# Pooled attention and a cosine-routed expert layer on one core: the expert chosen from the batch's mean value, and the work moved between passes and engines

## The chip, the cores and the metric

The kernel runs on one core of a Trainium2 chip. A core has five engines with queues of their own: TensorE (PE in the rows; its weight loads are PEld), VectorE (DVE), ScalarE (ACT), GpSimd (POOL) and SyncE (SP); transfers between HBM and the core's memory run on 16 DMA engines. The metric is the device time of one execution in microseconds (us), lower is better.

## What is computed

```python
def _attn_ref(q, k, v):                       # (8, 8, 576, 64)
    k_p = k.reshape(B, H, Sp, pool, D).mean(axis=3)      # pool = 8, Sp = 72
    v_p = v.reshape(B, H, Sp, pool, D).mean(axis=3)
    attn = softmax(scale * q @ k_p.T)
    return attn @ v_p
...
def _moe_ref(x, expert_emb, tau, w1, w2):     # x (4608, 512), 8 experts, F = 1024
    logits = xn @ en.T / tau                  # xn, en: rows of unit length
    expert_idx = np.argmax(logits, axis=1)
    gate_w = probs[np.arange(N), expert_idx]
    for e in range(E):
        mask = expert_idx == e
        h = np.maximum(x[mask] @ w1[e], 0.0)
        out[mask] = gate_w[mask, None] * (h @ w2[e])
```

The output of the attention, with the eight heads side by side, is the x of the expert layer. All inputs and the output are float32 in HBM; the loads turn them into fp16.

## The kernel before

**Batches and passes.** The work goes batch by batch, eight batches of 576 tokens. For each batch there is attention, and then one expert pass: all 576 tokens go through the one expert that the kernel takes for the batch's main one. `expert` (L299 to L317) routes tokens, counts which expert has most of them, and loads that expert's weights. Tokens of other experts would be handled in a loop at the end of the program (`For_i` and `If`), one more pass for each pair of batch and expert that the flags `pos_all` and `eb_all` show.

**Attention.** `kproc` (L158 to L172) adds neighbouring keys and transposes them, `qtr` (L181) transposes half of the queries, `vadd` (L190 to L195) adds groups of eight values into `vpx`; all three are VectorE's. `score` (L207, L213) is eight matmuls on TensorE and two exponentials on ScalarE; there are four a batch. `pv` (L227) is 48 small matmuls, `xtr` (L239 to L244) divides and transposes on VectorE into `xt_all`; there are three of each. `route` (L275 to L293) makes the logits and compares them on VectorE. `square` (L252, ScalarE), `sumsq` (L257, GpSimd), `ssq` (L265, six one-column matmuls, and a copy L269) and `norm` (L355, GpSimd) give the length of each token, and `prob` and `gate` (L359 to L378) the gate weight.

**Expert pass.** `hgrp` (L396) makes one of eight groups of the hidden layer in 8 matmuls of 288 columns; ScalarE brings it out of PSUM with a ReLU (L403), the sixth group VectorE (L405). `yblk` (L414) makes blocks of 128 tokens in 8 matmuls each, `ylast` (L437) the last 64 tokens. Blocks go out by VectorE (L427) and ScalarE (L425) in turn, the halves of the last one by one each (L443, L445). SyncE stores them (L469).

**Order.** Each engine works through its own queue in program order. The program order is made by `astream`: steps of all batches with a position in passes, sorted, and issued between the groups of the expert passes wherever the position is below `lead(b + done / total)`. Attention of a batch thus runs one to two passes ahead of its expert pass. All loads are issued by GpSimd, in order: inputs of a batch by `load_qkv` (L93 to L95, kk, qq, vv) from `more`, two batches ahead, and the two weight halves w1 and w2 by `load_w` (L100, L103) once the expert's index can be read. Input tiles have two buffers, weight tiles three, PSUM four.

Of the kernel before, what the change touches and what calls it, by code (L numbers as in the profile page):

```python
# [26 lines left out]
def kernel(  # L27
# [23 lines left out]
    NC = 5  # L51
# [45 lines left out]
    def load_w(e_val):  # L97
        w1 = wpool.tile([128, 4, F], FP16, name="w1")
        w2 = wpool.tile([128, 4, 2, DM], FP16, name="w2")
        nc.gpsimd.dma_start(  # L100
            out=w1,
            in_=moe_w1[ds(e_val, 1)].squeeze(0).rearrange("(p w) f -> p w f", w=4))
        nc.gpsimd.dma_start(  # L103
            out=w2,
            in_=moe_w2[ds(e_val, 1)].squeeze(0).rearrange(
                "(w p r) d -> p w r d", p=128, r=2))
        return w1, w2
# [42 lines left out]
    def attn_steps(b):  # L150
# [151 lines left out]
        def expert(cs, nfill=0):  # L302

            pc = psum()
            fill(pc[:, 512:704], nfill)
            count(cs, pc)
            mx = rt.tile([128, E], FP32, name="mx")
            nc.vector.max(out=mx, in_=pc[:, 0:E])
            ix = rt.tile([1, E], U32, name="ix")
            nc.vector.max_index(out=ix, in_max=mx[0:1], in_values=pc[0:1, 0:E])  # L310
            nc.vector.tensor_scalar(out=eb_all[:, b], in0=pc[:, 0:E], scalar1=mx[:, 0:1],
                                    scalar2=None, op0=ALU.is_ge)
            if len(cs) == NC:
                present(pc)
            e_val = nc.values_load(ix[0:1, 0:1], engines=[ENG.Pool], min_val=0,
                                   max_val=E - 1)
            weights[b] = load_w(e_val)  # L317
# [10 lines left out]

        routes[b] = st
# [17 lines left out]
        st['sumsq'], st['emit_ssq'] = sumsq, ssq
# [294 lines left out]
```

## Time and profile before

| | |
|---|---|
| median of 3 runs | 260.02 us (259.17 to 260.99) |
| the profiled execution | 259.8 us |
| its span, first to last instruction | 258.1 us |
| mean granted clock of TensorE | 0.915 |

A row of a group of instructions shows the line, engine, operation, output<-input, sizes and count; then busy time and mean duration of one (ns); then how long the engine stood idle ahead of them and which instruction ended most of that. A row of a stretch has its length, each engine's busy time (and count), the granted clock of TensorE (1.00 is 2.4 GHz, 0.50 is 1.2 GHz), the mean busy share of the 16 DMA engines and what they moved. A row of the chain has start, length and what ran. A row of the timeline has start, duration, engine, line and operation, and in brackets the idle time ahead and what ended it. A row of a load has the issuing engine, count, size as it lands and the time from issue to landing.

### The profile page before, as it was taken

To read this page: it belongs to the slowest core of one execution; us is meant where nothing else is said; L and a number is where in the kernel's file an instruction comes from. 1 tells how busy PE (TensorE), PEld (TensorE's weight loads), DVE (VectorE), ACT (ScalarE), POOL (GpSimd) and SP (SyncE) were. 2 spreads that over 40 slices of the span, in tenths; PEclk is the share of its full clock that TensorE was granted. 3 is DMA by queue.
4 is the path that set the end of the run, shared out by engine and by line. 5 is a ranking of instruction groups with operands and counts; after the bars stand their busy time and mean duration, and the time that the engine had idled before them with its cause. 6 is when DMAs were issued, how large, how long until landed. Compare 5 with 4: busy or idle time off the path is not lost.

```text
span 258.1 us, 6297 instructions
## 1 busy us (share of the span) xinstructions
PE 190.4 (74%) x2626; PEld 111.5 (43%) x2627; DVE 169.7 (66%) x361; ACT 107.4 (42%) x188; POOL 70.7 (27%) x75
## 2 busy tenths in 40 slices
PE   0235189096939986889598929898999999999930
PEld 0123146053416632664246603365556548657410
DVE  3774960977892989889967891989881494431210
ACT  3113129040637264548224633178339619325310
POOL 8204025042432126215430620116106113510000
PEclk9999999659977998899959986979999999999995
DMA  5998999879999738997999793239825965984140
GB/s 96 205 201 149 203 213 195 156 127 172 178 210 215 155 46 172 233 226 158 212 226 205 185 209 59 62 117 179 158 63 156 197 110 179 186 178 145 31 147 12
DMA packets 19583, 40.82 MB, mean 158 GB/s; under 512 B 2520, under 2 KB 8152, under 8 KB 18528
## 3 DMA queue, kind: packets, MB, share of 16 engines
q0 software_dynamic: 14096, 30.94, 65.9%
q1 hardware_dynamic: 5116, 8.86, 10.7%
q10 hardware_dynamic: 340, 0.59, 0.7%
q8 instruction: 21, 0.34, 0.5%
q14 instruction: 10, 0.08, 0.1%
HBM read 61.88 MB, written 9.44 MB: 276 GB/s over the span
## 4 chain that ended last, share of the span: by engine, by line
PE 37%; DVE 37%; DMA 12%; issue 4%; ACT 4%; POOL 1%; POOLq 0%; ACTq 0%
PE pa L396 15%; DMA vv<-in_v_dram 12%; PE pa L414 12%; DVE x_sb L241 6%; DVE xt_all L244 5%; DVE vv L190 4%; DVE vpx L195 4%; PE pa L227 3%; DVE kT L172 3%; DVE kk L158 3%; PE pa L437 2%; DVE qT L181 2%; PE pa L207 2%; PE pa L280 2%; DVE y_sb L427 2%
## 5 line engine op out<-in xcount | busy, mean ns | idle before, releaser
L396 PE MATMUL pa<-xt_all,w 128*128 128x288 f16 x512 | 74.2, 300 | 2.6 <-ACT y_sb L425 2.1
L414 PE MATMUL pa<-w,hT 128*128 128x512 f16 x256 | 66.6, 402 | 0.1
L396 PEld LDWEIGHTS <-w 128*128 128x128 f16 x512 | 49.9, 102 | 21.2 <-issue 6.0
L213 ACT ACTIVATE at<-pa 72x576 f16<-72x576 f32 x64 | 37.5, 643 | 27.8 <-PE pa L207 27.7
L403 ACT ACTIVATE hT<-pa 128x576 f16<-128x576 f32 x56 | 35.5, 648 | 16.6 <-PE pa L396 16.2
L207 PE MATMUL pa<-qT,kT 32*72 32x288 f16 x256 | 16.9, 330 | 30.1 <-DVE qT L181 13.1
L414 PEld LDWEIGHTS <-hT 128*128 128x128 f16 x256 | 23.3, 101 | 29.3 <-issue 8.3
L257 POOL TENSOR_TENSOR sq<-sq 128x1152 bf16<-128x1152 bf16 (+1 forms) x16 | 31.6, 1976 | 4.5 <-issue 3.8
L252 ACT ACTIVATE sq<-xt_all 128x576 bf16<-128x576 f16 x32 | 20.2, 673 | 25.8 <-DVE xt_all L244 24.9
L425 ACT ACTIVATE y_sb<-pa,gm 128x512 f32<-128x512 f32 x16 | 10.9, 683 | 45.8 <-DVE y_sb L427 40.5
L100 POOL DMA_DIRECT2D w<-in_moe_w_dram x8 | 4.8, 603 | 71.5 <-issue 23.8
L244 DVE STREAM_TRANSPOSE xt_all<-x_sb 128x768 f16<-128x768 f16 x24 | 23.5, 978 | 0.8
L207 PEld LDWEIGHTS <-kT 32*72 32x72 f16 x256 | 6.8, 116 | 39.6 <-issue 29.6
L241 DVE TENSOR_TENSOR x_sb<-pa,rc 128x768 f16<-128x768 f32 x24 | 23.0, 958 | 0.8
L355 POOL TENSOR_TENSOR ssq<-ssq,half_c 128x5 f32<-128x5 f32 x8 | 9.6, 1197 | 49.3 <-DVE ssq L269 49.3
L181 DVE STREAM_TRANSPOSE qT<-qq 128x1152 f16<-128x1152 f16 x16 | 21.7, 1362 | 0.0
L190 DVE TENSOR_TENSOR vv<-vv 72x2048 f16<-72x2048 f16 (+1 forms) x16 | 15.1, 947 | 9.3 <-DMA vv<-in_v_dram 9.0
L239 DVE RECIPROCAL rc<-pa 128x12 f32<-128x12 f32 x24 | 5.4, 226 | 22.7 <-PE pa L227 22.6
L227 PE MATMUL pa<-vpx,at 72*32 72x65 f16 x1152 | 15.6, 207 | 5.6 <-ACT y_sb L425 3.4
L227 PEld LDWEIGHTS <-at 72*32 72x32 f16 x1152 | 12.6, 104 | 14.6 <-issue 11.9
L427 DVE TENSOR_SCALAR y_sb<-pa,gm 128x512 f32<-128x512 f32 x16 | 11.7, 730 | 9.9 <-PE pa L414 9.9
L280 PE MATMUL pa<-enT,xt_all 128*128 128x8 f16 (+1 forms) x192 | 6.7, 172 | 14.8 <-DVE xt_all L244 14.6
(84 smaller groups left out, 159.5 us busy)
## 6 DMA issues: line engine op xcount, KB each, us to landing
w<-in_moe_w_dram POOLq DMA_DIRECT2D x16, 1024.0 KB, 11.8
out_dram<-y_sb SPq DMA_DIRECT2D x30, 256.0 KB
kk<-in_k_dram POOLq DMA_DIRECT2D x8, 576.0 KB, 12.0
vv<-in_v_dram POOLq DMA_DIRECT2D x8, 576.0 KB, 15.9
qq<-in_q_dram POOLq DMA_DIRECT2D x7, 576.0 KB, 12.4
out_dram<-y_sb SPq DMA_DIRECT2D x15, 64.0 KB
qq<-in_q_dram POOLq DMA_DIRECT2D x2, 288.0 KB, 8.1
out_dram<-y_sb ACTq DMA_DIRECT2D x2, 256.0 KB
```

What stands on the lines that cost most here:

```text
L181: nc.vector.transpose(out=qT.rearrange("p w r (t i) -> p t w r i", i=16), in_=qq.rearrange("p t (w r i) -> p t w r i", w=2, r=2))
L190: nc.vector.tensor_tensor(out=vv[:, :, 0:n], in0=vv[:, :, 0:n], in1=vv[:, :, n:2 * n], op=ALU.add)
L207: nc.tensor.matmul(out=pS[a // 2][0:G, (a % 2) * 512:(a % 2) * 512 + HALF], lhsT=kT[rows, w, r, :], rhs=qT[rows, w, r, :], start=(w == 0), ...
L213: nc.scalar.activation(out=at, in_=pS[i][0:G].rearrange("g (a c) -> g a c", a=2)[:, :, 0:HALF], func=AF.Exp, scale=escale)
L227: nc.tensor.matmul(out=px[ts(a, 32), c0:c0 + D + 1], lhsT=st['at', half, r, a // 2][:, a % 2, ts(blk, 32)], rhs=st['vpx'][:, 2 * a + r, 0: ...
L241: nc.vector.tensor_tensor(out=x_sb, in0=pxv[:, :, :, 0:D], in1=rc.unsqueeze(3).to_broadcast([128, 2, 6, D]), op=ALU.mult)
L244: nc.vector.transpose(out=xt_all[:, b].rearrange("p w (t l) -> p t w l", l=32)[:, ts(u, 6)], in_=x_sb.rearrange("p b j d -> p (b j d)").re ...
L252: nc.scalar.activation(out=st['sq'][:, w], in_=xt_all[:, b, w], func=AF.Square)
L257: nc.gpsimd.tensor_tensor(out=sq[:, 0:n], in0=sq[:, 0:n], in1=sq[:, n:2 * n], op=ALU.add)
L396: nc.tensor.matmul(out=ph[:, half * 512:half * 512 + HALF], lhsT=w1v[:, kk, w // 2, w % 2, :], rhs=xt()[:, kk, ts(half, HALF)], start=(kk ...
L403: nc.scalar.activation(out=dst, in_=src, func=AF.Relu)
L414: nc.tensor.matmul(out=py, lhsT=st['hT'][:, w // 2, w % 2, ts(c, 128)], rhs=w2[:, w // 2, w % 2, :], start=(w == 0), stop=(w == 7))
```

## The change

The main expert of a batch is no longer counted from routed tokens. `guess_sum` multiplies the summed values `vpx` by a column of ones (8 one-column matmuls), copies the sums over 128 columns, and `guess` multiplies them by the expert vectors (`enN`, 4 matmuls) and takes the largest. `weigh` then loads the weights. The routing of each token stays, as it makes the gate weights and the flags of the loop at the end. Positions are set by new tables: attention and routing inputs of batch b stand in pass b-1, the preparation of keys, queries and values in pass b-2, routing and gate of b at the start of pass b. `sumsq` is gone: `ssq` sums over the four parts by matmuls instead (24 a batch), and `square` makes 192 tokens of all four parts at once. All evacuations of the expert pass are on ScalarE, but for two blocks of the last batch. The hidden tile is split into two, the blocks of y are taken in a new order, and the first loads stand in a new order.

```diff
-    def load_w(e_val):
+    def load_w1(e_val):
         w1 = wpool.tile([128, 4, F], FP16, name="w1")
...
+    def load_w2(e_val):
         w2 = wpool.tile([128, 4, 2, DM], FP16, name="w2")
...
-        def square(w):
-            if w == 0:
-                st['sq'] = xp.tile([128, 4, S], BF16, name="sq", bufs=1)
-            nc.scalar.activation(out=st['sq'][:, w], in_=xt_all[:, b, w], func=AF.Square)
-
-        def sumsq():
-            sq = st['sq']
-            for n in (2, 1):
-                nc.gpsimd.tensor_tensor(out=sq[:, 0:n], in0=sq[:, 0:n], in1=sq[:, n:2 * n],
-                                        op=ALU.add)
...
             for c in (4, 0, 1, 2, 3):
-                for rows in token_rows(c):
-                    nc.tensor.matmul(out=pq[rows, c:c + 1],
-                                     lhsT=st['sq'][:, 0, cols(c)], rhs=ones_b,
-                                     start=True, stop=True)
+                for w in range(4):
+                    for rows in token_rows(c):
+                        nc.tensor.matmul(out=pq[rows, c:c + 1],
+                                         lhsT=st['sq'][:, w, cols(c)], rhs=ones_b,
+                                         start=(w == 0), stop=(w == 3))
...
+        def guess_sum():
+            pm = psum()
+            for h in range(H):
+                nc.tensor.matmul(out=pm[ts(h % 2, 64), h // 2:h // 2 + 1],
+                                 lhsT=st['vpx'][:, h, 0:D], rhs=ones_m[0:G, 0:1],
+                                 start=True, stop=True)
+            xb = rt.tile([128, 4, 128], FP16, name="xb")
+            (nc.scalar.copy if b < 2 else nc.vector.tensor_copy)(
+                out=xb, in_=pm[:, 0:4].unsqueeze(2).to_broadcast([128, 4, 128]))
+            st['xb'] = xb
+
+        def guess():
+            pg = psum()
+            for w in range(4):
+                nc.tensor.matmul(out=pg[:, 0:E], lhsT=st['xb'][:, w], rhs=enN[:, w, :],
+                                 start=(w == 0), stop=(w == 3))
             mx = rt.tile([128, E], FP32, name="mx")
...
+        def weigh():
+            weights[b] = load_w(chosen())
...
+        def square(u):
+            if u == 0:
+                st['sq'] = xp.tile([128, 4, S], BF16, name="sq", bufs=1)
+            cs = ts(u, 192)
+            nc.scalar.activation(out=st['sq'][:, :, cs], in_=xt_all[:, b, :, cs],
+                                 func=AF.Square)
...
-        L = [(-0.36, more)]
-        SC = [(0.28 + 0.12 * i, lambda h=i // 2, r=i % 2: score(h, r)) for i in range(4)]
...
+        L = [(d + 1.02, more)]
+        G_ = [(d + 1.12, guess_sum), (d + 1.18, guess)]
+        W = [(d + 1.185, weigh)]
...
+        SC = [(d + sd * i, lambda h=i // 2, r=i % 2: score(h, r)) for i in range(4)]
...
-            if w != 5:
-                nc.scalar.activation(out=dst, in_=src, func=AF.Relu)
-            else:
-                nc.vector.tensor_scalar(out=dst, in0=src, scalar1=0.0, scalar2=None,
-                                        op0=ALU.max)
+            nc.scalar.activation(out=dst, in_=src, func=AF.Relu)
...
-                if i % 2:
+                if i % 2 or not apart:
                     nc.scalar.activation(out=y_sb, in_=py, func=AF.Copy, scale=g)
...
+        order = [(0, 0), (1, 0), (0, 1), (1, 1), (2, 0), (3, 0), (2, 1), (3, 1)]
+        ysteps = [(0.87, lambda c=c, part=part: yblk(c, part)) for c, part in order]
+        ysteps.insert(2 if apart else 8, (0.87, ylast))
...
+    run(a0['K'], a0['Q'][:1], a0['S'][:2], a0['V'], a0['Q'][1:])
+    emb_transposed()
+    run(a0['G'])
+    e_val = routes[0]['chosen']()
+    w1 = load_w1(e_val)
+    nc.gpsimd.dma_start(out=qq1, in_=flat(q, 1))
+    weights[0] = w1, load_w2(e_val)
```

GpSimd's queue at the start of the program, before: the inputs of batch 1, then the index of batch 0 (`ix`), its two weight halves and the inputs of batch 2.

```order
L93 DMA kk_132<-in_k_dram 128x2304
L94 DMA qq_131<-in_q_dram 128x2304
L95 DMA vv_133<-in_v_dram 72x8x512
...
L315 TENSOR_LOAD ix_266
...
L100 DMA w1_279<-in_moe_w1_dram 128x4096
...
L103 DMA w2_280<-in_moe_w2_dram 128x4x1024
L93 DMA kk_314<-in_k_dram 128x2304
```

The same place of the changed kernel:

```order
L537 DMA vv_134<-in_v_dram 72x8x512
L538 DMA kk_133<-in_k_dram 128x2304
...
L326 TENSOR_LOAD ix_219
...
L96 DMA w1_234<-in_moe_w1_dram 128x4096
L561 DMA qq_132<-in_q_dram 128x2304
...
L103 DMA w2_237<-in_moe_w2_dram 128x4x1024
L90 DMA kk_322<-in_k_dram 128x2304
```

The first weight half stands ahead of the queries of batch 1 now; up to the second half the two queues hold the same loads.

GpSimd's queue in a middle pass, before: the two additions of the squares (`sq`), the inputs of batch 5, the power for the token lengths (`ssq`), and the index and weights of batch 2.

```order
L257 TENSOR_TENSOR sq_896<-sq_896 128x1152
L257 TENSOR_TENSOR sq_896<-sq_896 128x576
L93 DMA kk_1097<-in_k_dram 128x2304
L94 DMA qq_1096<-in_q_dram 128x2304
L95 DMA vv_1098<-in_v_dram 72x8x512
L355 TENSOR_TENSOR ssq_1183<-ssq_1183,half_c_97 128x5
L315 TENSOR_LOAD ix_1390
...
L100 DMA w1_1404<-in_moe_w1_dram 128x4096
```

A middle pass of the changed kernel (pass 2): the inputs of batch 5 and the weights of batch 3.

```order
L90 DMA kk_1542<-in_k_dram 128x2304
L91 DMA qq_1541<-in_q_dram 128x2304
L92 DMA vv_1543<-in_v_dram 72x8x512
L382 TENSOR_TENSOR ssq_1586<-ssq_1586,half_c_97 128x5
L326 TENSOR_LOAD ix_1649
...
L96 DMA w1_1664<-in_moe_w1_dram 128x4096
...
L103 DMA w2_1666<-in_moe_w2_dram 128x4x1024
```

The additions are gone, and the weights of a batch follow the inputs of the batch two further on.

VectorE's queue around the index of batch 3, before: the routing counts give the index (`mx`, `ix`), then come the value additions of batch 5.

```order
L308 MAX mx_1830<-pa_1823 128x8
L310 MAX_INDEX ix_1832<-mx_1830,pa_1823 1x8
L311 TENSOR_SCALAR eb_all_91<-pa_1823,mx_1830 128x8
L321 TENSOR_SCALAR pos_all_92<-pa_1823 1x8
L190 TENSOR_TENSOR vv_1098<-vv_1098 72x8x256
```

VectorE's queue around the index of batch 3 in the changed kernel:

```order
L194 TENSOR_TENSOR vv_614<-vv_614 72x8x256
L285 TENSOR_REDUCE lmax_1522<-pa_1495 128x5
...
L194 TENSOR_TENSOR vv_614<-vv_614 72x8x128
...
L199 TENSOR_TENSOR vpx_1527<-vv_614 72x8x64
L263 COPY ssq_1586<-pa_1561 128x5
L334 TENSOR_SCALAR pos_all_92<-pa_1598 1x8
L304 CAST xb_1616<-pa_1607 128x512
L316 MAX mx_1647<-pa_1642 128x8
L318 MAX_INDEX ix_1649<-mx_1647,pa_1642 128x8
```

The index now stands behind the value additions of its own batch instead of ahead of those of batch 5.

## Rows read from the trace of the kernel before

**Rows 1.** The page, busy us (share of the span) and instructions by engine

```profile
PE 190.4 (74%) x2626; PEld 111.5 (43%) x2627; DVE 169.7 (66%) x361; ACT 107.4 (42%) x188; POOL 70.7 (27%) x75
```

**Rows 2.** Chain that ended last, three pieces of it

```profile
23.16 21.76 DMA vv<-in_v_dram
44.95 1.23 DVE vv L190
...
247.39 0.69 ACT y_sb L425
```

**Rows 3.** Timeline: GpSimd's loads up to pass 1, and TensorE's first matmul there

```profile
37.88 0.85 POOL L95 DMA_DIRECT2D vv<-in_v_dram  x1
...
63.12 0.56 POOL L100 DMA_DIRECT2D w<-in_moe_w_dram  x1 [8.03 <-DVE rc L239]
...
72.77 1.14 PE L396 MATMUL pa<-xt_all,w 128*128 128x288 f16 x8 [1.53 <-ACT y_sb L425]
```

**Rows 4.** DMA issues: the loads issued at 37.88 and at 63.12

```profile
vv<-in_v_dram POOLq DMA_DIRECT2D x1, 576.0 KB, 15.7
...
w<-in_moe_w_dram POOLq DMA_DIRECT2D x1, 1024.0 KB, 8.6
```

**Rows 5.** Busy time by stage; at the end clock, DMA share, GB/s

```profile
23.10:53.60 30.50, 16.78 (x200) 9.96 (x201) 20.69 (x38) 10.45 (x19) 8.33 (x9) 0.89 0.99 182
58.00:71.80 13.80, 10.34 (x191) 5.38 (x190) 11.21 (x23) 4.16 (x7) 4.76 (x4) 1.00 0.98 180
72.77:81.00 8.23, 5.46 (x30) 3.19 (x30) 5.58 (x9) 3.92 (x7) 1.99 (x4) 0.59 1.05 205
108.00:118.00 10.00, 8.56 (x185) 6.46 (x183) 8.57 (x23) 6.10 (x12) 1.42 (x2) 1.00 1.03 222
108.00:136.00 28.00, 23.19 (x370) 13.16 (x369) 24.33 (x47) 13.56 (x24) 10.32 (x10) 0.88 1.00 208
193.45:214.75 21.30, 20.89 (x332) 12.59 (x329) 11.24 (x31) 13.13 (x25) 6.22 (x5) 1.00 0.72 156
231.16:247.40 16.24, 16.19 (x114) 10.03 (x112) 4.38 (x13) 6.88 (x13) 0.00 (x0) 1.00 0.32 99
```

**Rows 6.** Chain that ended last, one-column and eight-column matmuls, scores, hidden groups

```profile
84.57 0.31 PE pa L265 x6
...
91.54 0.78 PE pa L280 x24
...
198.37 0.37 PE pa L207 x8
...
231.22 7.95 PE pa L396 x64
```

**Rows 7.** Line 396, durations (min/median/max), first and last start

```profile
L396 PE MATMUL pa<-xt_all,w x512: 282/286/448, 37.5 to 238.9; 128*128 128x288 f16 x171
```

**Rows 8.** Groups by line, ScalarE and VectorE

```profile
L213 ACT ACTIVATE at<-pa 72x576 f16<-72x576 f32 x64 | 37.5, 643 | 27.8 <-PE pa L207 27.7
L403 ACT ACTIVATE hT<-pa 128x576 f16<-128x576 f32 x56 | 35.5, 648 | 16.6 <-PE pa L396 16.2
...
L252 ACT ACTIVATE sq<-xt_all 128x576 bf16<-128x576 f16 x32 | 20.2, 673 | 25.8 <-DVE xt_all L244 24.9 <-DVE z L370 0.8
...
L427 DVE TENSOR_SCALAR y_sb<-pa,gm 128x512 f32<-128x512 f32 x16 | 11.7, 730 | 9.9 <-PE pa L414 9.9
L425 ACT ACTIVATE y_sb<-pa,gm 128x512 f32<-128x512 f32 x16 | 10.9, 683 | 45.8 <-DVE y_sb L427 40.5 <-PE pa L414 5.3
...
L445 ACT ACTIVATE y_sb<-pa,gm 64x256 f32<-64x256 f32 x8 | 3.8, 469 | 7.2 <-DVE y_sb L443 7.0
```

**Rows 9.** Line 195, durations (min/median/max) of the value sum

```profile
L195 DVE TENSOR_TENSOR vpx<-vv x8: 420/422/3260, 14.2 to 172.7; 72x512 f16<-72x512 f16 x8
```

**Rows 10.** Timeline: GpSimd's additions and VectorE's value sum beside them

```profile
68.27 4.54 POOL L257 TENSOR_TENSOR sq<-sq 128x1152 bf16<-128x1152 bf16 x2 [3.81 <-issue]
...
68.87 2.47 DVE L195 TENSOR_TENSOR vpx<-vv 72x512 f16<-72x512 f16 x1
```

More of the change, by code (lines that the diff above doesn't have):

```diff
@@ L300, in count, with chosen @@
                                  rhs=oh_all[:, b, c], start=False, stop=(c == cs[-1]))
[L302 to L306, printed above, removed]
-            mx = rt.tile([128, E], FP32, name="mx")
[L308 to L317, printed above, removed]
+        def guess_sum():
[13 more added lines that the diff above has]
+                                 start=(w == 0), stop=(w == 3))
+            mx = rt.tile([128, E], FP32, name="mx")
+            nc.vector.max(out=mx, in_=pg[:, 0:E])
+            ix = rt.tile([128, E], U32, name="ix")
+            nc.vector.max_index(out=ix, in_max=mx, in_values=pg[:, 0:E])
+            ixf = rt.tile([128, 1], FP32, name="ixf")
+            nc.vector.tensor_copy(out=ixf, in_=ix[:, 0:1])
+            nc.vector.tensor_scalar(out=eb_all[:, b], in0=irow[:, 0:E], scalar1=ixf,
+                                    scalar2=None, op0=ALU.is_equal)
+            st['ix'] = ix
+        def chosen():
+            return nc.values_load(st['ix'][0:1, 0:1], engines=[ENG.Pool], min_val=0,
+                                  max_val=E - 1)
+        def weigh():
+            weights[b] = load_w(chosen())
         def present(pc):
@@ L379, in gate @@
             gates[b] = gm
-        return [st['sumsq'], st['emit_ssq'], norm, prob, gate]
+        return [st['emit_ssq'], norm, prob, gate]
     def ffn_steps(xt, get_w, get_gm, finish, apart=False):
@@ L442, in ylast @@
             g = get_gm()
-            nc.vector.tensor_scalar(out=y_sb[0:64, 0:DH], in0=py[0:64, 0:DH],
-                                    scalar1=g[0:64, 4:5], scalar2=None, op0=ALU.mult)
-            nc.scalar.activation(out=y_sb[64:128, 0:DH], in_=py[64:128, 512:512 + DH],
-                                 func=AF.Copy, scale=g[64:128, 4:5])
+            for r in range(2):
+                nc.scalar.activation(out=y_sb[ts(r, 64), 0:DH],
+                                     in_=py[ts(r, 64), r * 512:r * 512 + DH],
+                                     func=AF.Copy, scale=g[ts(r, 64), 4:5])
             finish(4, y_sb)
@@ L450, in ffn_steps @@
             steps.append((1.0, lambda w=w: hgrp(w)))
-        ysteps = [(0.87, lambda c=c, part=part: yblk(c, part))
-                  for c in range(4) for part in range(2)]
-        steps += [(0.87, ylast)] + ysteps if apart else ysteps + [(0.87, ylast)]
+        order = [(0, 0), (1, 0), (0, 1), (1, 1), (2, 0), (3, 0), (2, 1), (3, 1)]
+        ysteps = [(0.87, lambda c=c, part=part: yblk(c, part)) for c, part in order]
+        ysteps.insert(2 if apart else 8, (0.87, ylast))
+        steps += ysteps
         return steps
@@ L471, in store, with emb_transposed @@
         return finish
-    def emb_transposed(nfill):
-        pe = psum()
-        fill(pe[:, 512:704], nfill)
-        pe = pe.bitcast(FP16)
-        for w in range(4):
-            nc.tensor.transpose(out=pe[:, ts(w, E)], in_=emb_h[:, ts(w, 128)],
-                                identity=ident_h[:E, :E])
-        nc.vector.tensor_copy(out=enT, in_=pe[:, 0:4 * E].rearrange("p (w e) -> p w e", e=E))
+    def emb_transposed():
+        for i, dst in enumerate((enN, enT)):
+            pe = psum().bitcast(FP16)
+            for w in range(4):
+                nc.tensor.transpose(out=pe[:, ts(w, E)], in_=emb_h[:, i, ts(w, 128)],
+                                    identity=ident_h[:E, :E])
+            nc.vector.tensor_copy(out=dst,
+                                  in_=pe[:, 0:4 * E].rearrange("p (w e) -> p w e", e=E))
     with tc.manual_schedule():
@@ L491 @@
         nc.gpsimd.dma_start(out=qq0[:, 0:TH * D], in_=flat(q, 0)[:, 0:TH * D])
-        nc.gpsimd.dma_start(out=vv0, in_=grouped(v, 0))
-        nc.gpsimd.dma_start(out=qq0[:, TH * D:T * D], in_=flat(q, 0)[:, TH * D:T * D])
         nc.gpsimd.iota(icol, pattern=[[0, 1]], base=0, channel_multiplier=1,
@@ L497 @@
                        allow_small_or_imprecise_dtypes=True)
+        nc.gpsimd.dma_start(out=vv0, in_=grouped(v, 0))
+        nc.gpsimd.dma_start(out=qq0[:, TH * D:T * D], in_=flat(q, 0)[:, TH * D:T * D])
         nc.vector.tensor_scalar(out=ident_h, in0=irow, scalar1=icol, scalar2=None,
@@ L508 @@
             scalar1=-2.0 ** -14, scalar2=None, op0=ALU.mult)
-        nc.scalar.activation(out=emb_h, in_=emb, func=AF.Square, accum_out=emb_n)
+        nc.scalar.activation(out=emb_h[:, 0], in_=emb, func=AF.Square, accum_out=emb_n)
         nc.gpsimd.tensor_tensor(out=emb_n, in0=emb_n, in1=half_c[:E, 0:1], op=ALU.pow)
-        load_qkv(1)
+        qq1, kk1, vv1 = new_qkv(1)
+        nc.gpsimd.dma_start(out=vv1, in_=grouped(v, 1))
+        nc.gpsimd.dma_start(out=kk1, in_=flat(k, 1))
         nc.gpsimd.iota(pair_b, pattern=[[1, B], [0, E]], base=0, channel_multiplier=0)
@@ L557 @@
             for c, f in steps:
-                while j < len(astream) and astream[j][0] < lead(b + done / total):
+                while j < len(astream) and astream[j][0] < b + done / total + 1e-6:
                     astream[j][1]()
```

85 lines of the change are left out of this document (44 added, 41 removed).

## The prediction

> **What bounds the kernel now.** I read the busy line of the page first, then the chain that ended last, then the busy time by stage, then the timeline around the first loads. The profiled execution took 259.8 us: a span of 258.1 us and 1.7 us around it; the median of the three runs shown is 260.02 us. The sum below is made against the 259.8.
>
> TensorE is busy for 190.4 us and VectorE for 169.7 us of the span, ScalarE for only 107.4 [rows 1], so no engine fills it. The chain says where the rest is. It begins with transfers: a value load of 9.55 us, then one of 21.76 us that ends at 44.95, where VectorE's first value addition of batch 2 could begin [rows 2]. TensorE's next matmuls wait for what stands behind that addition in VectorE's order. The first matmul of expert pass 1 comes only at 72.77 [rows 3]. Its weights were issued at 63.12, as VectorE had to find the expert from finished attention first, and landed 8.6 us later, at 71.7 [rows 3, 4]. The last stages look otherwise: from 193.45 to 214.75 lies one whole pass with the attention of the next batch beside it, TensorE busy for 20.89 of 21.30 us at full clock; the last pass alone takes 16.24 us [rows 5]. So the end runs at TensorE's pace, while up to there late loads and VectorE's queue take time. Had all passes run as the last ones do, 72.77 plus six passes of 21.3 plus 16.24 plus the end (10.7 us after the last matmul, which ends at 247.39 [rows 2]) would make 227 us of span instead of 258.1.
>
> The loads have a bound of their own. Where the 16 DMA engines are full they move 182 GB/s (23.1 to 53.6 us, share 0.99), 180 (58 to 71.8), 208 (108 to 136) and at best 222 (108 to 118) [rows 5]; sizes are as they land, in half the width of what is read. A middle pass moves two weight halves of 1.049 MB, three inputs of 0.590 MB and 1.18 MB of output: 5.05 MB.
>
> **The change, part by part.**
>
> *Expert from the mean.* The expert's index now needs the values alone and no attention, so weights are asked for 0.8 pass before use, right behind the input loads of batch b+2. The index must be right, which no trace shows. Worked out from the reference's inputs, the mean value picks, in all eight batches, the expert that all 576 tokens pick; the nearest second is batch 2, 0.519 against 0.560. So no extra pass at the end. The chain it adds on TensorE is 12 small matmuls a batch. Six one-column matmuls take 0.31 us, 0.052 each, and 24 of eight columns 0.78 us [rows 6]: 0.6 us a pass.
>
> *First pass.* The preparation of batch 1, which stood inside batch 0's attention on VectorE, now comes behind it, and fewer bytes stand ahead of the first weight half. Pass 0 began at 37.5 us [rows 7]; I take 28 for it, an estimate, with 33 as the late end. With 22.8 us for a pass (below) it then ends near 51, at the latest 56. This decides nothing, as the next part shows.
>
> *Pass 1, set by the queue.* Before, everything up to the values of batch 3 (inputs 0 to 3 and weights 0) had landed at 37.88 + 15.7 = 53.6 us [rows 3, 4], with the DMA engines full all the way. The changed kernel puts the same bytes ahead of the first weight half of pass 1. Behind 53.6 come that half and about half of pass 0's output: 1.049 + 0.59 = 1.64 MB, 7.9 us at 208 GB/s. Pass 1 starts at 61.5, after a wait of TensorE of 5 to 10 us from the end of pass 0, and 11.3 us earlier than before (72.77).
>
> *Passes 1 to 4, set by the queue.* Each needs 5.05 MB: 24.3 us at 208 GB/s. TensorE needs less: the 21.30 us of the whole pass, plus 18 more one-column matmuls for the sum of squares (18 x 0.052 = 0.94, which GpSimd's additions did before), plus 0.6 for the mean: 22.8 us. So pass 5 starts at 61.5 + 4 x 24.3 = 158.7. That the queue has no gap I read from the order: the input loads wait only for VectorE's preparation of a batch two ahead, and cover the few us in which the index is found.
>
> *Passes 5 to 7, set by TensorE.* No inputs are left; 3.28 MB a pass need 15.8 us. Two passes, 22.8 and 22.2 (the latter without a mean): 45.0. The last pass: 16.24, plus 0.78 for routing, 1.24 for 24 one-column matmuls, 0.3 for the count: 18.6. The end stays 10.7, the rest around the span 1.7.
>
> **Sum: 61.5 + 97.2 + 45.0 + 18.6 + 10.7 + 1.7 = 234.7 us.** I take 235.
>
> *ScalarE takes VectorE's evacuations.* Per pass: 8 hidden groups (0.648), 8 exponentials (0.643), 4 blocks (0.683), 2 half blocks (0.469) and 3 squares; one of 768 elements is 0.83 by the slope between the 256- and 512-element rows from the 576-element row's 0.673 [rows 8]. With 0.3 for the gate that makes 16.7 us of 22.8: hidden, though not everywhere (see the rivals). VectorE loses eight hidden groups, 14 of 16 blocks at 0.730 us [rows 8], and the half blocks. Off the chain, I count it at nothing.
>
> *No GpSimd sums.* The value sum takes 0.42 us in the median, but up to 3.26 [rows 9]; one of 2.47 us began 0.60 us after a pair of GpSimd additions and ended inside it [rows 10]. This loss goes. VectorE then has some 18 us of work in a pass and is late nowhere, so this too is already in the 24.3 and not added.
>
> *A page against the queue's rate.* The saturated stretch moved 182 GB/s as landed, twice that as read [rows 5]. The Trainium skill, page "DMA: Bandwidth & Descriptors", section "Anatomy of one DMA — SWDGE (gpsimd) path", fits a transfer as about 2.0 us plus its bytes at 436 GB/s. By that, even counting bytes as read, a middle pass (7.73 MB in, 1.18 out) would need an estimated 20.4 us, less than TensorE, and rival B would be the forecast. This trace does not reach that rate in any full stretch, so I go by the rows.
>
> **The rivals.**
>
> *B, TensorE sets all passes.* If the queue holds 222 GB/s, a pass needs 22.7 us of it, TensorE's own 22.8. Then 61.5 + 5 x 22.8 + 22.2 + 18.6 + 12.4 = 228.7. For it: that rate stood for 10 us. Against: not for 28. Its lower end, with pass 1 at 59.4 (the weight half alone behind 53.6, at 182) and passes at 21.3 as before, is 59.4 + 127.8 + 17.6 + 12.4 = 217.2.
>
> *C, ScalarE sets the first half of a pass.* There a score group (0.37) and a hidden group (an eighth of 7.95, 0.99) give TensorE 1.36 us of work [rows 6] and ScalarE 2 x 0.643 + 0.648 = 1.93. If none of the 0.57 is caught up, four pairs cost 2.3 us a pass: 61.5 + 6 x 25.1 + 18.6 + 12.4 = 243. Against: four PSUM buffers, and hidden groups alone, which leave ScalarE 0.34 us each. The clock adds to this side: from 72.77 to 81.00, after TensorE's waits, the granted clock was 0.59, so mostly the lower level of 1.2 GHz, against 1.00 from 193 us on [rows 5]. The wait before pass 1 may cost a like stretch again.
>
> *D, the queue stays at 180 GB/s,* as from 58 to 71.8. A pass is 28.1 us: 61.5 + 112.4 + 45.0 + 18.6 + 12.4 = 249.9.
>
> *E, slower: the mean picks a wrong expert.* Every batch in which it does gets one more pass in the loop at the end, with nothing to hide it: weights 8.6 us to landing [rows 4], 16.24 of matmuls [rows 5], then up to 11.3 us to read 1.18 MB of output back and store it again at 208 GB/s: 25 to 36 us. From the first wrong batch it decides: 260 to 271. Here the change would not do what it says.
>
> *F, within 1%: the index comes late.* It now stands on VectorE behind its own batch's value additions, which wait for their load. If values land late, the weights are issued late into an empty queue; 4 us in each of six passes give 259. Against: these values are loaded a pass earlier than they are added.
>
> **Chances.** Forecast 0.47, B 0.22, C 0.13, D 0.11, E 0.03, F 0.04. All but E and F are faster than 257.4 us, so faster by over 1% (about what a measurement of this kernel can tell from no change) has 0.93, within 1% 0.04, slower 0.03. The range runs from just above B's lower end to D: 219 to 250.
>
> **What would show it.** Right: first expert matmul near 28 us, pass 1 near 61 behind a wait for its weights, passes 1 to 4 about 24 us apart with the DMA share near 1, then about 22.5, no GpSimd addition beside VectorE, no loop pass. Wrong: pass starts 22 to 23 us apart with no wait for weights (B); TensorE waiting for ScalarE in the first half of passes (C); DMA idle while TensorE waits for weights (F).

## The result, and the profile after

The changed kernel takes 237.47 us in the median of 4 runs (236.38 to 238.43), the kernel before 260.28 beside it: a ratio of 0.913 (95% interval 0.907 to 0.918). The forecast was 235.0, with a range of 219 to 250. The profiled execution took 237.07 us, of which the span is 235.4. (Of two kernels below, the one with both edits back and the kernel before with the edits alone, some executions were disturbed; the ratios leave these out.)

The busy line of the page, which answers to [rows 1]:

```profile
PE 188.3 (80%) x2862; PEld 115.9 (49%) x2863; DVE 140.8 (60%) x341; ACT 124.5 (53%) x212; POOL 40.0 (17%) x59
```

TensorE has 236 more instructions and is busy for 2.1 us less. VectorE lost 28.9 us and GpSimd 30.7. The chain that ended last (start, length, what ran), for [rows 2]:

```profile
3.03 9.33 DMA vv<-in_v_dram
...
44.24 15.88 DMA w<-in_moe_w_dram
...
92.57 15.91 DMA w<-in_moe_w_dram
...
116.89 19.19 DMA w<-in_moe_w_dram
```

The value load of 21.76 us is gone from it; the first one stays, with 9.33 us. From 44 us up to pass 4 it runs through three weight loads, which take 15.9 to 19.2 us from issue to use where [rows 4] had 8.6: they now stand in a full queue. TensorE's first expert matmuls of passes 1, 3 and 4 in the timeline (start, duration, in brackets the idle time ahead), for [rows 3], and three of VectorE's additions that end in the keys `kT`, for later:

```profile
60.16 2.10 PE L423 MATMUL pa<-xt_all,w 128*128 128x288 f16 x8 [8.51 <-DMA w<-in_moe_w_dram]
...
108.53 1.15 PE L423 MATMUL pa<-xt_all,w 128*128 128x288 f16 x8 [1.42 <-DMA w<-in_moe_w_dram]
...
136.12 1.14 PE L423 MATMUL pa<-xt_all,w 128*128 128x288 f16 x4 [4.68 <-DMA w<-in_moe_w_dram]
...
180.66 0.77 DVE L176 TENSOR_TENSOR kT<-k 128x128 f16<-128x128 f16 x3
```

Pass 1 starts at 60.16 instead of 72.77, and TensorE waits for weights there, as forecast. The stages (span of time, length, busy time and count of PE, PEld, DVE, ACT, POOL, granted clock, DMA share, GB/s), for [rows 5]: the wait before pass 1, passes 1 to 4, pass 5, pass 6, the last pass, and two short stretches behind waits.

```profile
51.65:60.16 8.51, 0.01 (x1) 0.00 (x0) 3.50 (x8) 0.64 (x2) 0.00 (x0) 0.75 1.08 232
60.16:161.15 100.99, 94.25 (x1420) 57.60 (x1421) 67.72 (x158) 60.49 (x104) 17.92 (x24) 0.90 1.00 204
161.15:184.23 23.08, 21.67 (x361) 13.61 (x358) 17.25 (x41) 15.21 (x27) 2.54 (x3) 1.00 0.71 159
184.23:205.93 21.70, 21.57 (x361) 13.46 (x358) 11.48 (x32) 15.20 (x27) 2.54 (x3) 1.00 0.71 153
205.93:222.82 16.89, 16.89 (x148) 10.68 (x145) 4.02 (x20) 7.59 (x13) 1.19 (x1) 1.00 0.23 70
59.00:62.00 3.00, 1.83 (x8) 1.04 (x8) 0.00 (x0) 0.00 (x0) 0.00 (x0) 0.50 1.09 236
137.00:140.00 3.00, 3.00 (x41) 1.68 (x39) 0.17 (x1) 1.74 (x3) 0.00 (x0) 0.50 1.09 206
```

In passes 1 to 4 the DMA engines are full (share 1.00, 204 GB/s). In the last three TensorE is busy for 60.1 of 61.7 us at full clock. Behind the waits of 8.51 and 4.68 us the granted clock stood at 0.50, which is 1.2 GHz. Last, the value sum of [rows 9] (minimum, median and maximum, ns):

```profile
L199 DVE TENSOR_TENSOR vpx<-vv x8: 420/422/423, 14.4 to 186.2; 72x512 f16<-72x512 f16 x8
```

The sum never takes more than 0.423 us now (3.26 before).

### The profile page after: what moved, and what is told of

Its sections match the earlier page's. It is cut to its first block, busy times and chain, and to the rows that moved or that the text cites. A ratio compares the mean times of both kernels' runs of the same rounds, so it can differ in the third digit from the quotient of the medians.

```text
span 235.4 us, 6749 instructions
## 1 busy us (share of the span) xinstructions
PE 188.3 (80%) x2862; PEld 115.9 (49%) x2863; DVE 140.8 (60%) x341; ACT 124.5 (53%) x212; POOL 40.0 (17%) x59
## 4 chain that ended last, share of the span: by engine, by line
PE 46%; DMA 30%; DVE 11%; ACT 4%; issue 3%; POOL 1%; POOLq 1%; ACTq 0%
DMA w<-in_moe_w_dram 22%; PE pa L423 21%; PE pa L437 12%; DMA qq<-in_q_dram 4%; DMA vv<-in_v_dram 4%; PE pa L211 3%; PE pa L231 3%; DVE qT L185 3%; PE pa L259 2%; PE pa L460 2%; ACT at L217 1%; DVE vv L194 1%; DVE xt_all L248 1%; DVE x_sb L245 1%; ACT hT L429 1%
## 5 line engine op out<-in xcount | busy, mean ns | idle before, releaser
L423 PE MATMUL pa<-xt_all,w 128*128 128x288 f16 x512 | 77.4, 303 | 14.9 <-DMA w<-in_moe_w_dram 14.6
L423 PEld LDWEIGHTS <-w 128*128 128x128 f16 x512 | 48.4, 102 | 33.8 <-DMA w<-in_moe_w_dram 14.9
L429 ACT ACTIVATE hT<-pa 128x576 f16<-128x576 f32 x64 | 41.4, 647 | 38.5 <-PE pa L423 38.5
L437 PE MATMUL pa<-w,hT 128*128 128x512 f16 x256 | 58.6, 380 | 0.1
L346 ACT ACTIVATE sq<-xt_all 128x768 bf16<-128x768 f16 x24 | 20.2, 843 | 29.5 <-DVE xt_all L248 27.1
L211 PE MATMUL pa<-qT,kT 32*72 32x288 f16 x256 | 16.8, 327 | 12.7 <-DVE qT L185 11.4
L448 ACT ACTIVATE y_sb<-pa,gm 128x512 f32<-128x512 f32 x30 | 18.9, 678 | 11.9 <-PE pa L437 11.9
L382 POOL TENSOR_TENSOR ssq<-ssq,half_c 128x5 f32<-128x5 f32 x8 | 10.5, 1306 | 81.8 <-DVE ssq L263 81.8
L263 DVE COPY ssq<-pa 128x5 f32<-128x5 f32 x8 | 1.3, 159 | 15.9 <-PE pa L259 15.9
L467 ACT ACTIVATE y_sb<-pa,gm 64x256 f32<-64x256 f32 x16 | 7.4, 464 | 2.3 <-PE pa L460 2.1
L460 PE MATMUL pa<-w,hT 128*64 128x256 f16 x128 | 8.5, 276 | 0.0
## 6 DMA issues: line engine op xcount, KB each, us to landing
w<-in_moe_w_dram POOLq DMA_DIRECT2D x16, 1024.0 KB, 15.4
qq<-in_q_dram POOLq DMA_DIRECT2D x7, 576.0 KB, 15.2
```

The costliest lines, as they stand in the source:

```text
L211: nc.tensor.matmul(out=pS[a // 2][0:G, (a % 2) * 512:(a % 2) * 512 + HALF], lhsT=kT[rows, w, r, :], rhs=qT[rows, w, r, :], start=(w == 0), ...
L346: nc.scalar.activation(out=st['sq'][:, :, cs], in_=xt_all[:, b, :, cs], func=AF.Square)
L423: nc.tensor.matmul(out=ph[:, half * 512:half * 512 + HALF], lhsT=w1v[:, kk, w // 2, w % 2, :], rhs=xt()[:, kk, ts(half, HALF)], start=(kk ...
L429: nc.scalar.activation(out=dst, in_=src, func=AF.Relu)
L437: nc.tensor.matmul(out=py, lhsT=st['hT', w // 4][:, (w // 2) % 2, w % 2, ts(c, 128)], rhs=w2[:, w // 2, w % 2, :], start=(w == 0), stop=(w ...
L448: nc.scalar.activation(out=y_sb, in_=py, func=AF.Copy, scale=g)
```

## The experiments

The total came out near the forecast. The open question was whether for the forecast's reasons: it put the whole gain down to the early expert and the load queue, and counted the two edits on engines (no evacuations on VectorE, no sums on GpSimd) at nothing. From here on "the two edits" are these. Two stretches of each profile are compared, passes 1 to 4 and passes 5 and 6, which in the changed kernel last 100.99 and 44.78 us (23.08 + 21.70).

### The two edits, without and with the rest of the change

First the kernel before with the two edits alone; its order of work and its choice of expert stay.

```diff
-            if w != 5:
-                nc.scalar.activation(out=dst, in_=src, func=AF.Relu)
-            else:
-                nc.vector.tensor_scalar(out=dst, in0=src, scalar1=0.0, scalar2=None, op0=ALU.max)
+            nc.scalar.activation(out=dst, in_=src, func=AF.Relu)
...
-            for n in (2, 1):
-                nc.gpsimd.tensor_tensor(out=sq[:, 0:n], in0=sq[:, 0:n], in1=sq[:, n:2 * n],
-                                        op=ALU.add)
+            pass
```

(Blocks of y go to ScalarE and the sum of squares to TensorE as in the change.)

> The kernel before with the two engine parts alone: all evacuations of the expert pass on ScalarE, sums of squares by 24 matmuls, no GpSimd additions; expert still from routing counts, order as before. Theory Q: 246 to 256 us: pass 1 still waits for weights that are asked for late (start near 70 us against 60), and the passes up to the fifth lose only VectorE's delays. Rival V: 240 us or less.

It took 243.88 us (242.78 to 247.93), 0.938 of before (0.932 to 0.944). That lies between the two ranges, but 6.2 of the whole change's 8.7% come without the early expert. Where, the stretch of passes 1 to 3 shows, first in the kernel before and then in this one:

```profile
72.77:169.86 97.09, 77.22 (x1172) 43.55 (x1172) 76.97 (x148) 44.03 (x78) 27.27 (x26) 0.88 0.82 168
```

```profile
71.82:153.55 81.73, 71.20 (x1244) 42.23 (x1245) 58.40 (x132) 49.15 (x89) 14.10 (x18) 0.98 0.96 202
```

Three passes are 15.4 us shorter. VectorE's 77.0 us of work become 58.4, and with VectorE on time the loads that wait for it are issued sooner. The first weight halves of passes 2, 3 and 4 are issued at 89.9, 112.7 and 133.8 us instead of 95.1, 119.1 and 144.4, and the DMA share goes from 0.82 to 0.96. Pass 1 still starts at 71.82 us. The whole change starts it 11.7 us earlier, at 60.16, and is 6.4 us faster than this kernel in the medians.

Then the other way round: the changed kernel with one edit undone, with the other, and with both. GpSimd's sums back (`sumsq` stands behind `square` again, `ssq` has six matmuls):

```diff
+        def sumsq():
+            sq = st['sq']
+            for n in (2, 1):
+                nc.gpsimd.tensor_tensor(out=sq[:, 0:n], in0=sq[:, 0:n], in1=sq[:, n:2 * n], op=ALU.add)
...
+        Z = [(pd + 0.285, sumsq)]
```

> The changed kernel with one part undone: GpSimd adds the squares again (2 additions a batch, right behind the last square) and TensorE's sum of squares has 6 one-column matmuls instead of 24. Theory Q (the load queue and TensorE set the end, VectorE has slack): 236 to 240 us, as VectorE's slower additions (15 us in all before) stay inside its slack and TensorE saves 18 x 0.052 = 0.9 us a pass in passes 5 to 7, the value sum again up to 3 us beside a GpSimd addition, pass 1 starting at 60 as now. Rival V (VectorE's relief carries the gain): 245 to 250 us.

243.95 us (243.34 to 245.42), ratio 0.940 (0.934 to 0.946), just under the range of V. VectorE's evacuations back (the sixth hidden group, every other block, half of the last):

```diff
-            nc.scalar.activation(out=dst, in_=src, func=AF.Relu)
+            if w != 5:
+                nc.scalar.activation(out=dst, in_=src, func=AF.Relu)
+            else:
+                nc.vector.tensor_scalar(out=dst, in0=src, scalar1=0.0, scalar2=None, op0=ALU.max)
...
-                if i % 2 or not apart:
+                if i % 2:
```

> The changed kernel with one part undone: VectorE again takes the sixth hidden group, two of four blocks and one half block of each pass, some 20 us of work in all. Theory Q: 235 to 240 us; VectorE goes from 141 to about 161 us busy and ScalarE from 124.5 to about 105, and neither is waited for. Rival V: 244 us or more, with TensorE waiting for VectorE's evacuations at pass ends.

247.25 us (246.1 to 248.06), ratio 0.951 (0.945 to 0.957), as V had it. Both back, by the two diffs together:

> The changed kernel with both engine parts undone (GpSimd sums and VectorE evacuations as before), so that the early expert and the new order stand alone. Theory Q: 237 to 244 us, pass 1 starting at 60 us, VectorE busy near 175 us. Rival V: 250 us or more.

Ratio 0.968 (0.961 to 0.975), as V had it, from executions of 250.8 and 252.27 us. Undoing the edits costs 6.5 us, 9.8 us and, both together, some 14. The early expert and the new order, which this last kernel has without the edits, bring 3.2%. No run parts the early expert from the new positions, the split hidden tile and the other smaller parts of the change. The stretches show where the loss lies, first with the sums back, then with the evacuations back, each time passes 1 to 4 and passes 5 and 6:

```profile
61.04:162.39 101.35, 93.10 (x1348) 56.16 (x1349) 73.69 (x156) 60.55 (x104) 33.42 (x32) 0.91 1.00 203
162.39:215.02 52.63, 46.25 (x680) 28.05 (x677) 33.52 (x74) 30.56 (x53) 12.45 (x10) 0.90 0.61 135
```

```profile
60.06:164.47 104.41, 97.49 (x1420) 59.02 (x1421) 75.15 (x171) 52.03 (x86) 17.92 (x24) 0.89 0.99 197
164.47:215.82 51.35, 48.02 (x716) 29.17 (x713) 35.60 (x83) 27.47 (x46) 5.09 (x6) 0.90 0.63 138
```

With the sums back, passes 1 to 4 take 101.35 us against 100.99: the full queue covers the loss. Passes 5 and 6 have no such cover and go from 44.78 to 52.63. With the evacuations back it is 3.4 and 6.6 us. In passes 5 and 6 the granted clock is 0.90 in both, 1.00 in the changed kernel. Most of the 6.6 us of the evacuations is not waiting: TensorE is idle there for 3.3 us instead of 1.5, but busy for 48.02 us instead of 43.24 with the same 716 instructions.

### What a GpSimd addition costs, and what a shared evacuation costs

Putting the sums back does two things: GpSimd's additions run beside VectorE, and the sums of squares wait for GpSimd. To part them, the same additions were put into a tile that nobody reads, while TensorE went on summing all four parts.

```diff
+        def scratch_sums():
+            sq, sc = st['sq'], att.tile([128, 2, S], BF16, name="sc", bufs=1)
+            nc.gpsimd.tensor_tensor(out=sc, in0=sq[:, 0:2], in1=sq[:, 2:4], op=ALU.add)
+            nc.gpsimd.tensor_tensor(out=sc[:, 0:1], in0=sc[:, 0:1], in1=sc[:, 1:2], op=ALU.add)
```

> The changed kernel with GpSimd's two additions of the squares put back, but into a tile that nobody reads; TensorE still sums over all four parts itself. Theory P (the additions hurt by what they do to VectorE's instructions beside them, keys' additions above all): most of the 6.5 us that putting the sums back cost comes again, 241 to 245 us, and the mean of the four additions that end in kT rises from 0.35 to 0.8 us or more. Rival S (what hurts is the wait of the sums of squares for GpSimd): 236.5 to 239 us.

246.49 us (244.77 to 247.17), ratio 0.947 (0.940 to 0.953): the additions alone cost 9.0 us, above even the range of theory P. That is more than the 6.5 us of the sums put back: there TensorE has 36 one-column matmuls fewer in passes 5 and 6, which take 52.63 us against 54.06 here, and the end was 1.9 us shorter. With the sums back TensorE also waited for GpSimd itself, twice and 4.3 us in all, but in passes 0 and 2, ahead of a wait for weights or under the full queue. The timeline of this kernel around one pass boundary, GpSimd's additions, then VectorE's queue and TensorE beside and behind them:

```profile
185.36 2.36 POOL L351 TENSOR_TENSOR sc<-sq 128x1152 bf16<-128x1152 bf16 x1 [10.11 <-ACT sq L346]
...
185.50 0.78 DVE L167 STREAM_TRANSPOSE k<-ks 128x576 f16<-128x576 f16 x1
...
186.31 3.14 DVE L176 TENSOR_TENSOR kT<-k 128x128 f16<-128x128 f16 x3
...
187.80 1.30 POOL L352 TENSOR_TENSOR sc<-sc 128x576 bf16<-128x576 bf16 x1
...
193.03 0.18 DVE L285 TENSOR_REDUCE lmax<-pa 128x5 f32<-128x40 f32 x1
...
193.61 0.90 PE L259 MATMUL pa<-ones_b,sq 128*64 128x1 bf16 x24 [2.21 <-DVE lg L287]
```

Three key additions take 3.14 us; in the changed kernel the same three take 0.77. Over all batches the mean of these additions is 0.94 us instead of 0.35. The transpose of the keys beside the same GpSimd addition keeps its 0.78. So VectorE is 2.4 us late; its reading of the routing logits (`lmax`, `lg`), which stands behind in its queue, is late, and TensorE waits 2.21 us for it. In the list of waits this is the largest entry behind the start of the program (total, times, longest), and in passes 5 and 6 the clock falls:

```profile
PE pa L259 <- DVE lg L287: 9.0, 4, 2.4
```

```profile
162.17:216.23 54.06, 48.52 (x716) 29.58 (x713) 33.39 (x74) 30.58 (x53) 12.44 (x10) 0.87 0.58 127
```

TensorE's own busy time is 48.52 us instead of 43.24 for the same 716 instructions, at 0.87 instead of 1.00, and it is idle for 4.0 us more. The Trainium skill, page "SBUF — State Buffer", section "SBUF: two separate sides", says that GpSimd and VectorE share a pair of ports under an exclusive lock, which an operation of VectorE with two inputs in SBUF needs while GpSimd reads SBUF. The trace agrees: the two-input additions are stretched over both GpSimd additions and end 0.35 us behind the second, the one-input transpose is not touched.

The second split: of the evacuations only the blocks of y were shared again, all hidden groups stayed on ScalarE.

```diff
-                if i % 2 or not apart:
+                if i % 2:
...
+            nc.vector.tensor_scalar(out=y_sb[0:64, 0:DH], in0=py[0:64, 0:DH],
+                                    scalar1=g[0:64, 4:5], scalar2=None, op0=ALU.mult)
```

> The changed kernel with only the output blocks shared with VectorE again (two of four, and half of the last); all eight hidden groups stay on ScalarE. Theory Y (blocks of one order that change from engine to engine make ScalarE wait behind VectorE's long instructions, and TensorE behind ScalarE): nearly all of the 9.8 us of the run with both parts put back, 244 to 248 us. Rival H (it is the hidden group in the middle of the eight that TensorE waits for): 236.5 to 240 us.

246.41 us (245.51 to 248.55), ratio 0.949 (0.942 to 0.957): theory Y, 8.9 of the 9.8 us. The timeline of this kernel at the start of pass 6:

```profile
187.93 2.63 DVE L185 STREAM_TRANSPOSE qT<-qq 128x1152 f16<-128x1152 f16 x2
...
190.48 0.71 DVE L450 TENSOR_SCALAR y_sb<-pa,gm 128x512 f32<-128x512 f32 x1
...
191.23 0.69 ACT L448 ACTIVATE y_sb<-pa,gm 128x512 f32<-128x512 f32 x1 [5.27 <-DVE y_sb L450]
...
191.97 0.31 PE L211 MATMUL pa<-qT,kT 32*72 32x288 f16 x2 [1.23 <-ACT y_sb L448]
```

VectorE's block stands behind the preparation of a later batch, here two transposes of the queries. ScalarE, whose block is the other half of the same PSUM tile, stands idle for 5.27 us until VectorE's is done, and TensorE waits for ScalarE. The stretch of passes 5 and 6 in this kernel:

```profile
163.79:215.66 51.87, 48.13 (x717) 29.50 (x715) 34.53 (x81) 28.68 (x48) 5.09 (x6) 0.90 0.62 136
```

It is 7.1 us longer than in the changed kernel. Only 2.2 us of that are idle time of TensorE; 4.9 us are its own busy time. Behind the wait of 1.23 us the granted clock stands at 0.50 from 193 to 199 us. So in this trace it is not the 0.71 us of work that costs, but the place in the queue and the clock behind the wait. No run tests why ScalarE's block waits for VectorE's, which reads the other half of the tile, or what the clock alone is worth here.

### The load queue

Is it the bytes in the queue that hold passes 1 to 4? The second weight half was loaded for pass 0 only.

```diff
-            weights[b] = load_w(chosen())
+            weights[b] = load_w1(chosen()), weights[0][1]
```

> The changed kernel with the second weight half loaded for pass 0 alone and used again in passes 1 to 7: 7 x 1.049 MB less to load, and the output of passes 1 to 7 is not the reference's. Everything else stands as it is. Theory Q (bytes in the queue hold passes 1 to 4): pass 1 still starts at 60 us, as its first half has the same bytes ahead; the waits of 1.4 and 4.7 us ahead of passes 3 and 4 go, passes take 22 to 23.5 us, total 228 to 232 us. Rival K (TensorE's own pace and its clock after waits hold them, bytes do not): 235 us or more.

225.3 us (223.32 to 226.53), ratio 0.867 (0.858 to 0.875), below the lower range. The same two stretches:

```profile
60.42:151.77 91.35, 90.18 (x1420) 55.74 (x1421) 67.62 (x158) 60.55 (x104) 14.90 (x20) 0.95 0.83 169
151.77:195.54 43.77, 43.24 (x716) 27.09 (x714) 28.64 (x72) 30.45 (x53) 3.57 (x4) 1.00 0.46 105
```

Passes 1 to 4 run in 91.35 us, TensorE is busy for 90.18 of them, and only the first waits for weights. So it is the bytes. Next the weights were issued ahead of the inputs of the batch two further on:

```diff
-        L = [(d + 1.02, more)]
+        L = [(d + 1.19, more)]
...
```

(The position for batch 1, which has a line of its own, moves likewise.)

> The changed kernel with one change of order: in each pass the weights of the next pass are issued ahead of the inputs of two batches on, not behind them. Same bytes, one set of inputs (1.77 MB, 8.5 us at 208 GB/s) less ahead of every weight half. Theory Q: pass 1 starts at 52 to 54 us instead of 60, waits ahead of passes 3 and 4 get short, total 228 to 232 us. Rival K: the wait ahead of pass 1 goes as well, but the gain stays below 4 us, 234 to 236 us, as later passes keep their lengths. Slower than 237 if the inputs now come too late for VectorE.

233.39 us (231.26 to 234.28), ratio 0.897 (0.889 to 0.905): between the two ranges. Pass 1 starts at 52.62 us, but four waits of 0.91 to 3.74 us for weights are left, ahead of passes 1, 2, 4 and 5, 8.0 us in all. And idle matmuls of 512 columns in place of the waits, 36, 6 and 18 at passes 1, 3 and 4, to hold the clock:

```diff
-        R = [(b + 0.0, lambda: route(0, NC)),
+        NF = {1: 36, 3: 6, 4: 18}.get(b, 0)
+        R = [(b + 0.0, lambda: [route(0, NC), NF and fill(psum()[:, 0:512], NF)]),
```

> The changed kernel with filler matmuls (512 columns, 36, 6 and 18 of them) behind the routing at the start of passes 1, 3 and 4, where TensorE now waits for weights, so that the engine does not go idle. No other change. Theory Q: the granted clock stays at 1.00 after the waits and pass 1 takes 22.8 instead of 24.6 us, but passes 3 and 4 still start when their weights land (108, 136): 234 to 238 us. Rival K: each half clock spell of 10 us costs 5, and most of it comes back: 228 to 233 us.

234.35 us (233.47 to 235.97), ratio 0.905 (0.898 to 0.912), the range of the queue. Then both together, 10, 5, 18 and 7 idle matmuls at passes 1, 2, 4 and 5:

> The weights stand ahead of the inputs, and idle matmuls are put in front of the hidden layer at the passes where TensorE waited for weights with that order: 10, 5, 18 and 7 of 512 columns (0.21 us each: 2.1, 1.1, 3.8, 1.5 us) at passes 1, 2, 4 and 5. Theory C (the short waits cost little themselves, the half clock behind each costs more): half-clock time between pass 0 and the last matmul falls from 30.7 us to about 10, half of which comes back: 223 to 229 us. Rival Q (the queue is what decides, the clock behind a wait is used up in later waits): the idle matmuls only stand where the waits stood, and the time stays at 231 to 235 us.

232.93 us (232.87 to 234.25), ratio 0.898 (0.893 to 0.904): rival Q, no gain that shows over the run without idle matmuls. Passes 1 to 4 with the idle matmuls alone, with the weights ahead alone, and with both:

```profile
60.30:160.76 100.46, 95.99 (x1444) 58.34 (x1445) 67.59 (x157) 60.52 (x104) 17.94 (x24) 0.95 1.00 203
```

```profile
52.62:156.03 103.41, 96.42 (x1421) 58.56 (x1421) 70.58 (x164) 61.24 (x104) 17.94 (x24) 0.88 1.00 210
```

```profile
52.82:155.78 102.96, 96.42 (x1452) 58.35 (x1450) 71.84 (x167) 60.90 (x104) 17.93 (x24) 0.95 1.01 212
```

The mean clock rises from 0.90 to 0.95 and the four passes take 100.46 us instead of 100.99; with the weights ahead it rises from 0.88 to 0.95, and 102.96 stand against 103.41. What TensorE saves, the idle matmuls and waits take up: where the queue decides, the lower clock cost at most some 0.5 us of 100 in these profiles. (The 3.1 us that the idle matmuls alone gained came later: 1.4 us in passes 5 and 6, and 1.8 us behind the last matmul, a time that varies from run to run.)

A last run went at the hole in the queue ahead of the first weights, by the load of the queries of batch 1, on top of both edits above:

```diff
         nc.gpsimd.dma_start(out=kk1, in_=flat(k, 1))
+        nc.gpsimd.dma_start(out=qq1, in_=flat(q, 1))
...
         w1 = load_w1(e_val)
-        nc.gpsimd.dma_start(out=qq1, in_=flat(q, 1))
```

> The kernel of the run before with weights ahead and idle matmuls (232.93 us), with one line moved: the load of batch 1's queries, which stood between the two halves of the first weights, is issued ahead of both, at 7.5 us instead of 20.5, where the DMA engines run dry (136, 96, 61 and 143 GB/s in the four stretches of 2 us from 16 to 24 us, which is 0.79 MB short of 208 GB/s; the queries have 0.59 MB). Theory Q (the sum of the queue's bytes decides when passes 1 to 4 can run): 0.59 MB / 208 GB/s = 2.8 us earlier from pass 1 on, 229 to 231.5 us. Rival T (TensorE and its clock decide by now, or the first weights land later for it): 232.5 to 235 us.

231.63 us (230.86 to 233.97), ratio 0.893 (0.887 to 0.898): between the two ranges, and not to be told from the run before. The stretch of the hole and one of pass 0, first without the edit and then with it:

```profile
16.00:24.00 8.00, 5.89 (x175) 3.40 (x175) 5.13 (x14) 3.68 (x6) 3.73 (x6) 1.00 0.66 109
40.00:44.50 4.50, 4.43 (x118) 2.44 (x116) 3.29 (x10) 2.46 (x5) 0.00 (x0) 1.00 0.90 149
```

```profile
16.00:24.00 8.00, 6.26 (x175) 3.50 (x175) 5.13 (x14) 3.69 (x6) 3.22 (x5) 1.00 0.98 190
40.00:44.50 4.50, 4.50 (x96) 2.22 (x81) 3.77 (x10) 2.00 (x4) 0.38 (x1) 1.00 0.30 51
```

The hole is filled (109 to 190 GB/s), and a new one opens at 40 us (149 to 51): the next loads wait for the index of batch 1, which came only 0.5 us earlier, so pass 1 began at 52.35 instead of 52.82. Of the 2.8 us moved, 0.5 stayed. Its interval lies below that of the changed kernel. Of the kernels that do the whole work it has the lowest median, though the intervals of the two others with the weights ahead overlap its own.

### The end

The end behind the last matmul had grown from 10.7 to 12.6 us, and the order of the last blocks of y is part of the change, so the last pass got the kernel before's order back.

```diff
-        ysteps.insert(2 if apart else 8, (0.87, ylast))
+        if apart:
+            ysteps = [(0.87, lambda c=c, part=part: yblk(c, part))
+                      for c in range(4) for part in range(2)]
+        ysteps.insert(0 if apart else 8, (0.87, ylast))
```

> The changed kernel with the last pass alone in the order of before: the 64 last tokens first, then the blocks one after the other, so that one block and not two is finished at the very end. Theory: the 12.6 us behind the last matmul become 10.7 as before, total 235 to 236.5 us. Rival (the end is the program's closing and not the stores): no change, 237 us.

237.2 us (236.3 to 237.66), ratio 0.915 (0.909 to 0.920): no change, as the rival had it. The end took 12.0 us in it; over all runs it took 10.5 to 12.8, the shortest (with GpSimd's sums back) with the changed kernel's own order. Why it varies stays open.

## Why the prediction was right, and where it was not

Against the profiled execution the terms came out as follows: pass 1 at 60.16 us (61.5 forecast); passes 1 to 4 in 101.0 (97.2); passes 5 and 6 in 44.8 (45.0); the last pass 16.9 from its first hidden matmul (18.6, which held the routing that lies ahead of it); the end 12.6 (10.7); around the span 1.7 (1.7). The errors of -1.3, +3.8, -0.2, -1.7 and +1.9 nearly cancel: before rounding they leave the 2.4 us between 234.7 and 237.07. That they cancel is luck.

**Right: the queue sets pass 1 and passes 1 to 4.** Pass 1 waits for weights behind a full queue, and halving the weight loads shortened these passes by 9.6 us. The term was mis-sized by 3.8 us: 204 GB/s for 101.0 us is 20.6 MB, where the sum had 20.2 MB at 208. Rival B's 222 GB/s did not come, nor did rival D's 180. The prediction's estimate from the Trainium skill, page "DMA: Bandwidth & Descriptors", section "Anatomy of one DMA — SWDGE (gpsimd) path", was 20.4 us of the queue for a pass. The trace does not agree: a pass took 25.2 us with the queue full.

**Right, but as a bare assumption: the passes at TensorE's pace.** 45.0 us for passes 5 and 6 was taken from a pass of the kernel before in which VectorE had only 11.24 us of work [rows 5]. In the changed kernel pass 5 holds the preparation of batch 7 beside it. That TensorE kept its pace there, 44.78 us, it owes to the two edits: with one or the other undone it is 52.63 or 51.35.

**Wrong: the two edits at nothing.** The step that failed is "Off the chain, I count it at nothing" for the evacuations, and for the sums "late nowhere, so this too is already in the 24.3 and not added". The second half of that holds for passes 1 to 4 alone, where 101.35 us with the sums back is 101.0 without. In passes 5 and 6 the sums cost 7.9 us (6.5 in the whole kernel, as its end was 2.1 us shorter), and the evacuations 6.6 there and 3.4 before. By the forecast's working a change without the two edits would have come out near 235 as well; it takes some 251. And the two edits alone took the kernel before to 243.88 us, where the forecast had nothing for them. The rows that spoke against it were there: ScalarE stood idle for 45.8 us ahead of its blocks of y, 40.5 of them until VectorE's block was done [rows 8], and the value sum took 2.47 us beside GpSimd [rows 10]. The first was not read for this at all, the second as a loss of VectorE's beside TensorE's work; the runs show that TensorE waits behind both.

**The clock.** It was named with rival C as a stretch that "may" cost. It was there, 0.50 behind the waits of 8.51 and 4.68 us, but inside passes that the queue sets it cost next to nothing (0.5 us of 100). In passes 5 and 6, when VectorE makes TensorE wait, TensorE's busy time grows by 4.8 us with the evacuations back; no run tests the clock by itself there.

**The other rivals.** TensorE hardly waits for ScalarE (no wait above 0.7 us in the changed kernel, C), no pass was added at the end (16 weight loads, two for each batch, E), and the index came in time: the DMA engines were full (share 1.08) while TensorE waited for weights (F). ScalarE's 15.2 us in each of passes 5 and 6 lie hidden, below the 16.7 of the forecast (whose own terms add up to 16.8).

## What to carry to other kernels

Work on an engine "off the chain" costs nothing only as long as what stands behind it in that engine's queue is not awaited: follow the queue to the next reader of a PSUM tile before an edit is counted at nothing, and count it stage by stage, as undoing the same edit was nearly free under a full load queue and cost 8 us where TensorE sets the pace. Where two engines take turns on one output, the one with the shorter queue waits for the other, and its readers with it. And a total that comes out right proves no term of the sum: undo the parts one by one.

## What the runs showed of the hardware that was not expected

GpSimd additions of 3.7 us a pass whose result nobody reads made three VectorE additions take 3.14 us instead of 0.77, and the kernel 9.0 us slower. In passes 5 and 6 of that kernel 4.0 us more of idle time came with a mean granted clock of 0.87 instead of 1.00, and the same 716 instructions of TensorE took 5.3 us longer: more than the waits themselves. A wait of TensorE of 1.23 us, in the kernel with shared blocks of y, had 6 us at a granted clock of 0.50 behind it. With the DMA share at 1.00 or 1.01 over 100 us, the engines moved 203 to 212 GB/s, output stores included, in each order of the loads that was run.
